# Zero-padded query pairs, untiled scores, a late LN factor, four shared PSUM banks and reordered loads in a chunked-attention and MLP kernel

## The chip, the cores and the metric

The kernel runs on one core of a Trainium2 chip. The metric is the device time of one execution in microseconds (us). Matrix work is done by TensorE (PE, with its weight loads listed as PEld), the rest by VectorE (DVE), ScalarE (ACT) and GpSimd (POOL). DMAs are issued here from POOL (loads from DRAM, which also convert fp32 to fp16) and from SyncE's queue (SP: copies inside the on-chip memory SBUF, and the output).

## The reference

Attention over chunks of 32 positions. Each chunk sees 8 memory keys, 16 positions to its left, itself, and 8 to its right. The result, with the 8 heads of 64 side by side, is the x of a LayerNorm and a two-layer MLP with a residual:

```
B, H, S, D = 4, 8, 768, 64;  chunk, left, right = 32, 16, 8;  n_mem = 8
for each chunk c:
    k_full = concat(mem_k, k[c_start-left : c_end+right]);  v_full likewise
    a = softmax(q_c @ k_full.T / sqrt(D))
    out[c] = a @ v_full
x   = out as (B, S, 512)
xn  = (x - mean(x)) / sqrt(var(x) + 1e-6) * g_ln
y   = x + max(xn @ w_ch1, 0) @ w_ch2          # w_ch1 512 x 2048, w_ch2 2048 x 512
```

## The kernel before

**Attention.** A batch is cut into 12 groups of two chunks (64 queries). For each group, `KT` (L56) holds columns of a block of 72: the left halo, the memory keys, the keys of the group; a score product takes 128 columns from the start of a block and uses 104 of them (KR). `kq_block` (L164) turns two heads of K and Q at a time with 32 PE transposes of 96 rows (L171) into a PSUM tile `att`, of which there are two, each two banks; DVE copies the K half to `KT` (L178), ACT the Q half to `QT` (L182). `scores` (L187) makes, for one group, eight products with a contraction of 64: the even head of a pair lies in rows 0 to 63 and the odd head in rows 64 to 127 of the PE array (tile_position, L194-L199). Each group takes one `att` tile, and two exps of 256 columns (L201) add a band bias that masks what a chunk must not see; the first and the last group have their own biases. `values` (L207) handles two groups (128 positions, tile t): 16 products with V (L213), whose 65th column of ones gives the sums; a reciprocal (L220) and a product (L221) make x, bn_stats and bn_aggr (L228, L229) mean and variance, and four POOL operations (L230 to L241) the normalized xn: minus the mean, plus eps, the power of -1/2, and the pass over x. `turn_x` (L246) transposes xn on PE and copies it to `xT`.

**V.** `V` (L55) has rows for the left halo (0 to 15), the memory values (16 to 23 and 88 to 95), the group (24 to 87) and the right halo (96 to 103). `load_v` (L100) issues one DMA per group from POOL; halos and memory rows are then copied inside SBUF from SP's queue (`load_v_halo`, `load_v_mem`).

**MLP.** The work is cut into eight stages u of 384 positions (three tiles). `up(u, hc)` (L261) makes 128 hidden units with four products of 384 columns (L264) in one of two banks `f1p`; the ReLU goes to `rT` on DVE for even hc (L273) and on ACT for odd hc (L271). `down(u, i, part)` (L279) adds four of the sixteen products of an output tile (L284) in one of two banks `f2p`; after part 3, DVE adds x (L292) and SP issues the output (L293). `scale_w1` (L137) multiplies w1 by g once, 16 passes on DVE (L139).

**Order.** Every engine works through its instructions in the order in which the program writes them. L296 to L363 write the start: batch 0's loads, the identity and masks on POOL, memory keys, four blocks, attention of three tiles, all four `scale_w1`, and the loads of batch 1. Then each stage has 28 steps (L367 to L398): 16 ups, then 12 downs, tile after tile. A plan adds work behind a step: for the next stage's tile i, scores at step 1+7i, values at 5+7i, turn_x at 10+7i; in even stages the four blocks of the next batch at steps 3, 7, 11, 17 and the loads of k and q of the batch after it at step 20; in odd stages V of that batch (12 DMAs from POOL at step 2), its memory columns of KT (on POOL, L158), and the halos. So xn on POOL (L241) stands in one queue with all loads from DRAM.

Of the kernel before, what the change touches and what calls it, by code (L numbers as in the profile page):

```python
# [15 lines left out]
def kernel(  # L16
# [12 lines left out]
    nc = tc.nc  # L29
# [7 lines left out]
    HD = 65  # L37

# [9 lines left out]
    band = sb.tile([128, 3, 2], FP32, name="band")  # L48
    zero6 = sb.tile([128, 3, 2], FP32, name="zero6")
    mhalf = sb.tile([128, 3], FP32, name="mhalf")  # L50
# [6 lines left out]
    QT = [sb.tile([128, 4, S], FP16, name=f"QT{i}") for i in range(2)]  # L57
    AT = [sb.tile([128, H, 64], FP16, name=f"AT{i}") for i in range(4)]
# [6 lines left out]
    mv = [sb.tile([128, 2], FP32, name=f"mv{i}") for i in range(3)]  # L65
    lnc = [sb.tile([128, 3], FP32, name=f"lnc{i}") for i in range(3)]
# [3 lines left out]
    f1p = [ps.tile([128, 384], FP32, name=f"f1p{i}") for i in range(2)]  # L70
    f2p = [ps.tile([128, 512], FP32, name=f"f2p{i}") for i in range(2)]
    turn = {"att": 0, "f1": 0, "f2": 0}

    def slot(kind):
        lst = {"att": att, "f1": f1p, "f2": f2p}[kind]
        turn[kind] = (turn[kind] + 1) % len(lst)
        return lst[turn[kind]]
# [15 lines left out]
    def load_kq(b):  # L93
        for dst, src in ((k16, k), (q16, q)):
            nc.gpsimd.dma_start(
                out=dst[b % 2][:, :, :, :],
                in_=dram(src, b * H * HS, [[512, 96], [HS, H], [1, 512]]),
            )

    def load_v(b, g0, g1):  # L100
        vt = V[b % 2]
        for g in range(g0, g1):
            nc.gpsimd.dma_start(  # L103
                out=vt[24:88, g, :, 0:64],
                in_=dram(v, b * H * HS + 64 * g * D, [[64, 64], [HS, H], [1, 64]]),
            )

    def load_v_halo(b, g0, g1):

        vt = V[b % 2]  # L110
        lo = max(g0, 1)
        nc.sync.dma_start(out=vt[0:16, lo:g1, :, :], in_=vt[72:88, lo - 1 : g1 - 1, :, :])
        hi = min(g1, NG - 1)
        nc.sync.dma_start(out=vt[96:104, g0:hi, :, :], in_=vt[24:32, g0 + 1 : hi + 1, :, :])

    def load_v_mem(b):
# [14 lines left out]
    def load_w2(c):  # L131
        nc.gpsimd.dma_start(
            out=w2c[c],
            in_=dram(moe_w_ch2, c * 512 * 512, [[512, 128], [128 * 512, 4], [1, 512]]),
        )
# [20 lines left out]
    def mem_cols(b):  # L156
        src = memKT[:, 4 * b : 4 * b + 4, :]
        nc.gpsimd.tensor_copy(  # L158
# [5 lines left out]
    def kq_block(b, j):  # L164

        p = slot("att")
        for half, src in ((0, k16), (1, q16)):
            pv = as16(p[:, half, :])
            for r in range(8):
                for par in range(2):  # L170
                    nc.tensor.matmul(  # L171
                        out=pv[64 * par : 64 * par + 64, 96 * r : 96 * r + 96],
                        lhsT=src[b % 2][:, 2 * j + par, r, :], rhs=identity[0:96, 0:96],
                        is_transpose=True, start=True, stop=True,
                        tile_position=(0, 64 * par),
                    )
        pk, pq = as16(p[:, 0, :]), as16(p[:, 1, :])
        nc.vector.tensor_copy(  # L178
            out=free(KT[b % 2], j * KC + 24, [[BLK, NG], [8, 8], [1, 8]]),
            in_=free(pk, 0, [[8, NG], [1, 8], [96, 8]]),  # L180
        )
        nc.scalar.copy(  # L182
            out=free(QT[b % 2], j * S, [[8, 96], [1, 8]]),
            in_=free(pq, 0, [[1, 96], [96, 8]]),
        )

    def scores(b, t):  # L187
        for g in (2 * t, 2 * t + 1):
            cls = 0 if g == 0 else 2 if g == NG - 1 else 1
            p = slot("att")  # L190
            a = AT[g % 4]
            for j in range(4):
                for par in range(2):
                    nc.tensor.matmul(  # L194
                        out=p[:, par, 64 * j : 64 * j + 64],
                        lhsT=KT[b % 2][64 * par : 64 * par + 64, j, BLK * g : BLK * g + 128],
                        rhs=QT[b % 2][64 * par : 64 * par + 64, j, 64 * g : 64 * g + 64],
                        start=(j == 0), stop=(j == 3), tile_position=(64 * par, 0),
                    )  # L199
            for c in range(2):  # L200
                nc.scalar.activation(  # L201
                    out=free(a, 32 * c, [[64, 2], [128, 4], [1, 32]], KR),
                    in_=free(p, 32 * c, [[512, 2], [64, 4], [1, 32]], KR),
                    func=ACTF.Exp, bias=band[0:KR, cls, c : c + 1], scale=0.125,
                )

    def values(b, t, x):  # L207
        p = slot("att")
        for h in range(H):
            for gg in range(2):  # L210
                g = 2 * t + gg
# [3 lines left out]
                    lhsT=AT[g % 4][0:KR, h, :],  # L215
                    rhs=V[b % 2][0:KR, g, h, :],
# [9 lines left out]
        )  # L226
        i = t % 3
        nc.vector.bn_stats(out=bst[i], in_=x)  # L228
        nc.vector.bn_aggr(out=mv[i], in_=bst[i])  # L229
        nc.gpsimd.tensor_scalar(  # L230
            out=lnc[i][:, 0:1], in0=mv[i][:, 0:1], scalar1=-1.0, scalar2=1.0,
            op0=ALU.mult, op1=ALU.mult,
        )
# [195 lines left out]
```

## Time and profile before

| | |
|---|---|
| median of three runs | 303.1 us (302.35 to 304.27) |
| profiled execution, its own time | 303.64 us |
| its span in the profile | 301.9 us |
| PE busy, share of the span | 226.7 us, 75% |
| DVE, POOL, ACT busy | 124.1, 92.4, 79.6 us |
| mean granted PE clock | 0.955 |

The profile is that of one execution. Times in its rows count from the start of the span. In a timeline row stand start, length, engine, line, operation, output <- inputs, shapes and count; in brackets the idle time before it and what ended it. A row with x8 merges eight instructions, and its length reaches to the modelled end of the last, so that the time from one row's start to the next row's start is the better price. Rows of groups end in busy time, mean ns of one, idle time before, and the releaser.

### The profile page before, as it was taken

What the parts mean: (1) busy time and instruction counts of PE and PEld (TensorE: products, weight loads), DVE (VectorE), ACT (ScalarE), POOL (GpSimd) and SP (SyncE); (2) the same over time, 40 slices, a digit from 0 to 9 for tenths busy, and PEclk for the clock granted to TensorE, in tenths of its full rate; (3) what the DMA queues carried; (4) which work ended last, traced back from release to release, by engine and by line L of the source; (5) the groups of instructions that cost most, each with busy time, mean ns of one, the idle gap of its engine ahead of it and who ended that gap; (6) DMA issues with size and microseconds to landing.
All of it is one profiled execution on the core that took longest, in us unless ns stands there. A gap on an engine that the chain in (4) does not pass through costs nothing.

```text
span 301.9 us, 5523 instructions
## 1 busy us (share of the span) xinstructions
PE 226.7 (75%) x2288; PEld 122.4 (41%) x2288; DVE 124.1 (41%) x253; ACT 79.6 (26%) x177; POOL 92.4 (31%) x185
## 2 busy tenths in 40 slices
PE   0073136289997059999998079989998999899994
PEld 0072022145554024455444034455444544444541
DVE  2042374065435015375535034375435445543311
ACT  1026103035224003055314012155224304321300
POOL 8194476250290332210291522220212220221000
PEclk9999999879999759999999759999999999999999
DMA  6999999992069990100169990100010011011001
GB/s 79 169 125 184 157 200 173 147 55 39 35 115 190 83 48 29 64 28 2 37 102 207 86 54 35 72 2 2 35 72 0 3 71 37 0 38 69 0 37 69
DMA packets 41978, 22.26 MB, mean 74 GB/s; under 512 B 27752, under 2 KB 38760, under 8 KB 41880
## 3 DMA queue, kind: packets, MB, share of 16 engines
q0 software_dynamic: 36896, 13.70, 67.5%
q1 hardware_dynamic: 5056, 8.19, 9.9%
q8 instruction: 18, 0.29, 0.5%
q14 instruction: 8, 0.07, 0.1%
HBM read 27.40 MB, written 6.29 MB: 112 GB/s over the span
## 4 chain that ended last, share of the span: by engine, by line
PE 57%; DMA 17%; POOL 8%; DVE 8%; issue 5%; ACT 2%; DVEq 0%; POOLq 0%; ACTq 0%
PE f2p L284 26%; PE f1p L264 23%; DMA q<-in_q_dram 13%; DMA w1c<-in_moe_w_ch_dram 4%; PE att L213 3%; PE att L171 2%; PE att L250 2%; PE att L194 2%; DVE bst L228 2%; DVE xs L221 2%; POOL V L103 2%; DVE KT L178 2%; POOL xn L241 1%; ACT QT L182 1%; POOL lnc L238 1%
## 5 line engine op out<-in xcount | busy, mean ns | idle before, releaser
L264 PE MATMUL f1p<-xT,w1c 128*128 128x384 f16 x512 | 101.4, 341 | 8.9 <-DVE rT L273 5.3
L284 PE MATMUL f2p<-w2c,rT 128*128 128x512 f16 x384 | 87.8, 379 | 0.0
L271 ACT ACTIVATE rT<-f1p 128x384 f16<-128x384 f32 x64 | 31.7, 496 | 151.8 <-PE f1p L264 151.7
L264 PEld LDWEIGHTS <-w1c 128*128 128x128 f16 x512 | 48.9, 101 | 46.0 <-issue 18.9
L273 DVE TENSOR_SCALAR rT<-f1p 128x384 f16<-128x384 f32 x64 | 35.2, 550 | 41.6 <-PE f1p L264 41.5
L284 PEld LDWEIGHTS <-rT 128*128 128x128 f16 x384 | 35.7, 98 | 39.5
L103 POOL DMA_DIRECT2D V<-in_v_dram x48 | 32.3, 685 | 37.8 <-DMA q<-in_q_dram 13.9
L230 POOL TENSOR_SCALAR lnc<-mv 128x1 f32<-128x1 f32 x24 | 4.6, 192 | 127.5 <-DVE mv L229 127.5
L201 ACT ACTIVATE AT<-att,band 104x256 f16<-104x256 f32 x96 | 37.6, 480 | 9.5 <-PE att L194 9.5
L250 PE MATMUL att<-identity,xn 128*128 128x128 f16 x96 | 10.5, 239 | 31.7 <-POOL xn L241 31.6
L292 DVE TENSOR_TENSOR osb<-f2p,xs 128x512 f32<-128x512 f32 x24 | 16.6, 692 | 40.8 <-PE f2p L284 40.8
L255 DVE COPY xT<-att 128x512 f16<-128x512 f16 x24 | 10.1, 420 | 46.2 <-PE att L250 46.2
L182 ACT COPY QT<-att 128x768 f16<-128x768 f16 x16 | 12.8, 800 | 46.4 <-DVE KT L178 46.4
L178 DVE COPY KT<-att 128x768 f16<-128x768 f16 x16 | 15.3, 956 | 17.0 <-PE att L171 17.0
L250 PEld LDWEIGHTS <-xn 128*128 128x128 f16 x96 | 6.5, 104 | 38.9 <-POOL xn L241 38.1
L241 POOL TENSOR_SCALAR xn<-xs,lnc 128x512 f16<-128x512 f32 x24 | 18.9, 786 | 2.6
L221 DVE TENSOR_TENSOR xs<-att,rec 128x512 f32<-128x512 f32 x24 | 16.6, 691 | 1.0 <-DVE rec L220 0.2
L228 DVE BATCH_NORM_STATS2 bst<-xs 128x6 f32<-128x512 f32 x24 | 16.7, 694 | 0.8
L194 PE MATMUL att<-QT,KT 64*128 64x64 f16 x384 | 11.6, 198 | 5.6 <-ACT QT L182 3.8
L238 POOL TENSOR_TENSOR lnc<-lnc,mhalf 128x1 f32<-128x1 f32 x24 | 13.4, 558 | 2.0
L194 PEld LDWEIGHTS <-KT 64*128 64x128 f16 x384 | 8.1, 98 | 13.5 <-issue 13.1
L213 PEld LDWEIGHTS <-AT 104*64 104x64 f16 x384 | 9.0, 120 | 10.5 <-issue 8.5
(36 smaller groups left out, 91.8 us busy)
## 6 DMA issues: line engine op xcount, KB each, us to landing
out_dram<-osb SPq DMA_DIRECT2D x24, 256.0 KB, 2.0
k<-in_k_dram POOLq DMA_DIRECT2D x4, 768.0 KB, 9.1
q<-in_q_dram POOLq DMA_DIRECT2D x4, 768.0 KB, 14.2
V<-in_v_dram POOLq DMA_DIRECT2D x48, 64.0 KB, 12.5
w1c<-in_moe_w_ch_dram POOLq DMA_DIRECT2D x4, 512.0 KB, 9.6
w2c<-in_moe_w_ch_dram POOLq DMA_DIRECT2D x4, 512.0 KB, 13.9
V<-memv SPq DMA_DIRECT2D x8, 97.5 KB
V<-V SPq DMA_DIRECT2D x3, 178.8 KB
```

What stands on the lines that cost most here:

```text
L103: nc.gpsimd.dma_start(out=vt[24:88, g, :, 0:64], in_=dram(v, b * H * HS + 64 * g * D, [[64, 64], [HS, H], [1, 64]]),)
L178: nc.vector.tensor_copy(out=free(KT[b % 2], j * KC + 24, [[BLK, NG], [8, 8], [1, 8]]), in_=free(pk, 0, [[8, NG], [1, 8], [96, 8]]),)
L194: nc.tensor.matmul(out=p[:, par, 64 * j : 64 * j + 64], lhsT=KT[b % 2][64 * par : 64 * par + 64, j, BLK * g : BLK * g + 128], rhs=QT[b % 2 ...
L201: nc.scalar.activation(out=free(a, 32 * c, [[64, 2], [128, 4], [1, 32]], KR), in_=free(p, 32 * c, [[512, 2], [64, 4], [1, 32]], KR), func= ...
L221: nc.vector.tensor_tensor(out=x.rearrange("p (a h d) -> p a h d", a=2, h=4), in0=free(p, 0, [[512, 2], [HD, 4], [1, 64]]), in1=free(r, 0, ...
L228: nc.vector.bn_stats(out=bst[i], in_=x)
L241: nc.gpsimd.tensor_scalar(out=xn[i], in0=x, scalar1=lnc[i][:, 0:1], scalar2=lnc[i][:, 2:3], op0=ALU.add, op1=ALU.mult,)
L250: nc.tensor.matmul(out=pv[:, 128 * dt : 128 * dt + 128], lhsT=xn[i][:, 128 * dt : 128 * dt + 128], rhs=identity, is_transpose=True, start= ...
L264: nc.tensor.matmul(out=p, lhsT=w1c[hc // 4][:, dt, 128 * (hc % 4) : 128 * (hc % 4) + 128], rhs=xT[u % 2][:, dt, :], start=(dt == 0), stop= ...
L271: nc.scalar.activation(out=rT[u % 2][hc], in_=p, func=ACTF.Relu)
L273: nc.vector.tensor_scalar(out=rT[u % 2][hc], in0=p, scalar1=0.0, scalar2=None, op0=ALU.max)
L284: nc.tensor.matmul(out=p, lhsT=rT[u % 2][hc][:, 128 * i : 128 * i + 128], rhs=w2c[hc // 4][:, hc % 4, :], start=(hc == 0), stop=(hc == 15),)
```

## The change

- **Scores.** Q goes to `QZ`: for each group and pair of heads 128 columns, the even head's 64 with zeros in rows 64 to 127, the odd head's 64 with zeros in rows 0 to 63. One product with all 128 rows then gives both heads' scores: four per group without tile_position instead of eight with it. `scores` does both groups of a tile in one `att` tile, with two exps of 512 columns. ACT copies Q in two halves of 64 rows. The zeros are cleared once at the start by DVE. One band bias is left: for the first and last group the rows outside the sequence have zeros in V and in its ones column (`tail1`).
- **LN.** xn is x minus the mean only. The factor (var + 1e-6)^(-1/2) is made in `root` on POOL and multiplied in at the output (ReLU lets a positive factor of a row through): L292 becomes one scalar_tensor_tensor. In the first stages the subtraction is done by DVE, later by POOL (`on_pool`).
- **MLP.** `f1p` and `f2p` become four shared banks `mm`. `rT` is kept once instead of twice. w2 is loaded with 2048 contiguous elements per partition, so hidden unit 4p+i of a part lies at place (p, i), and `up` takes its weights from w1 with a step of four elements.
- **Loads and order.** K, Q of batches 0 and 1 are loaded and turned in two parts (rows 0 to 63, then 64 to 95; CUT); V of batches 2 and 3 is loaded in eight DMAs by head, spread over steps of stages 2 and 4; the identity and masks are written ahead of V's loads; `mem_cols` moves from POOL to DVE; `scale_w1` 1 to 3 move into stage 0; the steps of stages 0, 1 and 2 get their own plan.

The diff, cut to its core:

```
-    QT = [sb.tile([128, 4, S], FP16, name=f"QT{i}") for i in range(2)]
-    AT = [sb.tile([128, H, 64], FP16, name=f"AT{i}") for i in range(4)]
+    QZ = [sb.tile([128, 4, NG, 2, 64], FP16, name=f"QZ{i}") for i in range(2)]
+    AT = [sb.tile([128, 2, H, 64], FP16, name=f"AT{i}") for i in range(3)]
-    rT = [[sb.tile([128, 384], FP16, name=f"rT{i}_{hc}") for hc in range(16)] for i in range(2)]
+    rT = [sb.tile([128, 384], FP16, name=f"rT{hc}") for hc in range(16)]
-    f1p = [ps.tile([128, 384], FP32, name=f"f1p{i}") for i in range(2)]
-    f2p = [ps.tile([128, 512], FP32, name=f"f2p{i}") for i in range(2)]
+    mm = [ps.tile([128, 512], FP32, name=f"mm{i}") for i in range(4)]
...
     def mem_cols(b):
-        nc.gpsimd.tensor_copy(
+        nc.vector.tensor_copy(
...
-        nc.scalar.copy(
-            out=free(QT[b % 2], j * S, [[8, 96], [1, 8]]),
-            in_=free(pq, 0, [[1, 96], [96, 8]]),
-        )
+        for par in range(2):
+            rows = slice(64 * par, 64 * par + 64)
+            o = free(QZ[b % 2][rows, j, g0, par, :], 0, [[128, ng], [8, 8], [1, 8]])
+            i = free(pq[rows, :], 0, [[8, ng], [1, 8], [n, 8]])
+            nc.scalar.copy(out=o, in_=i)
...
+        p = slot("att")
+        a = AT[t % 3]
+        for gg in range(2):
+            g = 2 * t + gg
             for j in range(4):
+                nc.tensor.matmul(
+                    out=p[:, gg, 128 * j : 128 * j + 128],
+                    lhsT=KT[b % 2][:, j, BLK * g : BLK * g + 128],
+                    rhs=QZ[b % 2][:, j, g, :, :],
+                    start=True, stop=True,
+                )
+        for c in range(2):
+            nc.scalar.activation(
+                out=free(a, 32 * c, [[512, 2], [64, 8], [1, 32]], KR),
+                in_=free(p, 32 * c, [[512, 2], [64, 8], [1, 32]], KR),
+                func=ACTF.Exp, bias=band[0:KR, c : c + 1], scale=0.125,
+            )
...
+        if on_pool:
...
+            root(t, xi)
+        else:
+            nc.vector.tensor_scalar(
+                out=xn[i], in0=x, scalar1=m[:, 0:1], scalar2=None, op0=ALU.subtract,
+            )
...
     def up(u, hc):
+        p = slot("mm")[:, 0:384]
+        c, i = hc // 4, hc % 4
         for dt in range(4):
+            w = w1c[c][:, dt, :]
             nc.tensor.matmul(
+                out=p, lhsT=free(w, i, [[4, 128]]), rhs=xT[u % 2][:, dt, :],
...
-            nc.vector.tensor_tensor(out=o, in0=p, in1=xs[t % 9], op=ALU.add)
+            nc.vector.scalar_tensor_tensor(
+                out=o, in0=p, scalar=rstd[t % 9], in1=xs[t % 9], op0=ALU.mult, op1=ALU.add,
+            )
...
+        if u == 0:
+            for c in range(1, 4):
+                at(4 * c - 2, scale_w1, c)
             for j in range(4):
+                at(15, kq_block, 0, j, CUT, 96)
+            attend(((15, 16, 19), (15, 17, 21), (16, 18, 23)))
+            at(24, mem_cols, 1)
+            at(24, v_mem, 1)
+        elif u == 1:
+            for j in range(4):
+                at(10 + j, kq_block, 1, j, 0, CUT)
+            at(12, v_before, 1, 1, 6)
+            at(12, v_after, 1, 0, 5)
+            attend(((16, 20, 24), (18, 22, 26), (20, 24, 27)))
+            for which in range(2):
+                at(24, load_kq, 1, which, CUT, 96)
+            for g in range(6, NG):
+                at(25, load_v_group, 1, g)
...
+            for which in range(2):
+                at(27, load_kq, 2, which)
+        elif u + 1 < NU:
+            attend(tuple((1 + 7 * i, 5 + 7 * i, 10 + 7 * i) for i in range(3)))
+            if u == 2:
+                plan.clear()
+                for j in range(4):
+                    at(j, kq_block, 1, j, CUT, 96)
+                attend(((5, 10, 15), (9, 14, 19), (13, 18, 24)))
+                for j in range(4):
+                    at((17, 20, 22, 25)[j], kq_block, 2, j)
...
+            if u in (2, 4):
+                bn = u // 2 + 1
+                for h in range(H):
+                    at(6 + 2 * h, load_v_head, bn, h)
+                at(24, mem_cols, bn)
+                at(24, v_mem, bn)
+                at(27, v_before, bn, 1, NG)
+                at(27, v_after, bn, 0, NG - 1)
+            if u == 3:
+                for which in range(2):
+                    at(2 + which, load_kq, 3, which)
         for step in range(28):
             if step < 16:
                 up(u, step)
+            elif u == 0:
+                down(u, (step - 16) % 3, (step - 16) // 3)
             else:
                 down(u, (step - 16) // 4, (step - 16) % 4)
```

At the start the new order is: on POOL the loads of mem_k and of rows 0 to 63 of k and q, the identity, the masks, V of groups 0 to 5 and its right halo, w1, the rest of k and q, V of groups 6 to 11, w2; on DVE the clears of V, KT and QZ, then `tail1`; then memory keys and columns, four blocks of rows 0 to 63, attention of three tiles with one `scale_w1` between the second and the third xT.

More of the change, by code (lines that the diff above doesn't have):

```diff
@@ L132, in load_w2 @@
         nc.gpsimd.dma_start(
-            out=w2c[c],
-            in_=dram(moe_w_ch2, c * 512 * 512, [[512, 128], [128 * 512, 4], [1, 512]]),
+            out=w2c[c], in_=dram(moe_w_ch2, c * 512 * 512, [[2048, 128], [1, 2048]])
         )
@@ L162, in mem_cols, with kq_block @@
         )
-    def kq_block(b, j):
+    def kq_block(b, j, lo=0, hi=96):
+        n, g0, ng = hi - lo, lo // 8, (hi - lo) // 8
         p = slot("att")
@@ L187, in scores @@
     def scores(b, t):
[L188 to L191, printed above, removed]
+        p = slot("att")
+        a = AT[t % 3]
+        for gg in range(2):
+            g = 2 * t + gg
             for j in range(4):
[L193 to L204, printed above, removed]
-                )
@@ L208, in values @@
+    def values(b, t, xi, on_pool):
+        x = xs[xi]
         p = slot("att")
@@ L284, in down @@
             nc.tensor.matmul(
-                out=p, lhsT=rT[u % 2][hc][:, 128 * i : 128 * i + 128],
+                out=p, lhsT=rT[hc][:, 128 * i : 128 * i + 128],
                 rhs=w2c[hc // 4][:, hc % 4, :],
@@ L372, in at, with attend @@
             plan.setdefault(step, []).append((fn, args))
-        if u + 1 < NU:
-            for i in range(3):
+        def attend(i_steps):
+            for i, (s0, s1, s2) in enumerate(i_steps):
                 t = 3 * half + i
-                at(1 + 7 * i, scores, b1, t)
-                at(5 + 7 * i, values, b1, t, xs[(3 * (u + 1) + i) % 9])
-                at(10 + 7 * i, turn_x, u + 1, i)
-        if u % 2 == 0 and u // 2 + 1 < B:
-            bn = u // 2 + 1
-            for j in range(4):
-                at((3, 7, 11, 17)[j], kq_block, bn, j)
-            if bn + 1 < B:
-                at(20, load_kq, bn + 1)
```

247 lines of the change are left out of this document (138 added, 109 removed).

## The prediction

> **What bounds the kernel now.** I read the busy times by stage first. A stage u runs from its first up product to the next stage's; the eight follow each other, columns being window, length, busy time (with counts) of PE, PEld, DVE, ACT, POOL, then granted clock, DMA share, GB/s.
>
> ```profile
> 47.70:87.50 39.80, 32.40 (x349) 17.15 (x349) 15.58 (x29) 11.32 (x24) 14.24 (x27) 0.91 0.91 85
> 87.50:126.40 38.90, 26.42 (x222) 13.32 (x221) 12.67 (x26) 8.20 (x20) 12.38 (x24) 0.87 1.41 93
> 126.40:155.90 29.50, 28.44 (x349) 15.69 (x348) 16.13 (x30) 11.20 (x24) 7.98 (x16) 1.00 0.11 31
> 155.90:193.50 37.60, 27.15 (x221) 13.75 (x220) 12.88 (x26) 8.20 (x20) 12.38 (x24) 0.86 1.28 96
> 193.50:223.10 29.60, 28.56 (x350) 15.75 (x349) 16.13 (x30) 11.20 (x24) 5.11 (x12) 1.00 0.08 28
> 223.10:249.50 26.40, 24.90 (x222) 12.87 (x221) 12.58 (x26) 8.20 (x20) 5.12 (x12) 1.00 0.08 31
> 275.90:301.90 26.00, 21.99 (x113) 10.74 (x111) 7.19 (x12) 3.93 (x8) 0.00 (x0) 1.00 0.11 41
> ```
>
> Stage 6 equals stage 5. Undisturbed stages (4 to 7) are bound by PE. Stages 1 and 3 have stage 5's work but last 38.9 and 37.6 against 26.4 us: 23.7 us lost, with the clock at 0.87. The chain that ended last says to what:
>
> ```profile
> 3.00 11.55 DMA q<-in_q_dram
> ...
> 153.82 14.32 DMA q<-in_q_dram
> ...
> 172.86 0.54 POOL KT L158
> ...
> 174.56 0.78 POOL xn L241
> 175.39 0.61 PE att L250 x4
> ```
>
> POOL issues loads in order and then makes xn. A V load stands until q has landed, xn behind it, and PE behind xn. The start, by the timeline, loses more:
>
> ```profile
> 14.84 0.67 POOL L103 DMA_DIRECT2D V<-in_v_dram  x1 [3.83 <-DMA q<-in_q_dram]
> 16.06 0.09 DVE L311 MEMSET memv<- 8x32 f16 x1 [11.86 <-DMA memv<-in_mem_v_dram]
> 16.14 0.56 PE L149 MATMUL att<-identity,memk 8*128 8x8 f16 x16 [16.14 <-POOL identity masks.py:199]
> 21.46 0.68 SPq L114 DMA_DIRECT2D V<-V  x1
> 28.82 0.65 PE L213 MATMUL att<-V,AT 104*64 104x65 f16 x16 [1.74 <-DMA w1c<-in_moe_w_ch_dram]
> 37.71 0.77 POOL L241 TENSOR_SCALAR xn<-xs,lnc 128x512 f16<-128x512 f32 x1
> 41.87 5.47 DVE L139 TENSOR_SCALAR w1c<-w1c,g_col 128x512 f16<-128x512 f16 x16
> 47.72 2.72 PE L264 MATMUL f1p<-xT,w1c 128*128 128x384 f16 x8 [2.79 <-DVE xT L255]
> 51.87 0.67 POOL L103 DMA_DIRECT2D V<-in_v_dram  x1 [1.33 <-DMA w2c<-in_moe_w_ch_dram]
> 59.27 0.85 PE L171 MATMUL att<-identity,q 96*64 96x96 f16 x16 [3.77 <-DMA q<-in_q_dram]
> ```
>
> The identity waits behind a V load until 15.8; first xn stands behind w2 issues until 37.7; four w1 scalings (5.47) stand in DVE ahead of the last xT; then stage 0 waits for batch 1's k and q. At 51.87 a V load comes free on a w2 load: all of w2 has landed.
>
> **Inside a stage** the PE timeline prices everything:
>
> ```profile
> 129.49 0.53 PE L171 MATMUL att<-identity,k 96*64 96x96 f16 x16
> ...
> 130.30 1.47 PE L264 MATMUL f1p<-xT,w1c 128*128 128x384 f16 x8
> ...
> 223.06 1.46 PE L264 MATMUL f1p<-xT,w1c 128*128 128x384 f16 x8
> 224.46 0.41 PE L194 MATMUL att<-QT,KT 64*128 64x64 f16 x16
> 224.80 2.96 PE L264 MATMUL f1p<-xT,w1c 128*128 128x384 f16 x16
> 227.69 0.45 PE L213 MATMUL att<-V,AT 104*64 104x65 f16 x16
> ...
> 230.69 0.81 PE L264 MATMUL f1p<-xT,w1c 128*128 128x384 f16 x4 [1.14 <-DVE rT L273]
> ...
> 246.63 0.40 PE L250 MATMUL att<-identity,xn 128*128 128x128 f16 x4
> 246.87 2.75 PE L284 MATMUL f2p<-w2c,rT 128*128 128x512 f16 x12
> ...
> 275.86 11.67 PE L264 MATMUL f1p<-xT,w1c 128*128 128x384 f16 x64
> 287.37 10.52 PE L284 MATMUL f2p<-w2c,rT 128*128 128x512 f16 x48
> ```
>
> I count from one start to the next. A down product takes 10.52/48 = 0.219 us; three quarters of its width 0.164, so 64 up products 10.5. They take 11.5 in stage 7.
>
> **Part by part.**
>
> *Four shared banks.* I read that 1.0 us as waits for the two f1 banks, besides the 1.14 and some 0.4 us of visible waits in stages like 5. With four banks an eviction may be late by three up groups (2.0 us), more than the values chain holds DVE. Gain 1.0 in stage 7, about 1.9 elsewhere. The single set of rT costs nothing: rT's first four are last read three down groups (2.6 us) before the next stage rewrites them.
>
> *Scores.* Sixteen tiled products take 0.34 us. Four untiled 128-wide ones with their own loads take 0.24 (the transposes), so eight 0.48: +0.14 per pair, 24 pairs, +3.4. The Trainium skill (TensorEngine Tiling (Array Packing), When to Use Tiling) recommends row tiling for a contraction of 64, up to twofold: by it the pair would cost 0.68 and the sum be some 5 us more; the transposes' row decides. ACT's half as many, twice as wide exps cost no more (rows below), off PE.
>
> *Zero-padded Q* doubles ACT's copies:
>
> ```profile
> L264 PEld LDWEIGHTS <-w1c 128*128 128x128 f16 x512 | 48.9, 101 | 46.0 <-issue 18.9
> L201 ACT ACTIVATE AT<-att,band 104x256 f16<-104x256 f32 x96 | 37.6, 480 | 9.5 <-PE att L194 9.5
> L271 ACT ACTIVATE rT<-f1p 128x384 f16<-128x384 f32 x64 | 31.7, 496 | 151.8 <-PE f1p L264 151.7
> L228 DVE BATCH_NORM_STATS2 bst<-xs 128x6 f32<-128x512 f32 x24 | 16.7, 694 | 0.8
> L182 ACT COPY QT<-att 128x768 f16<-128x768 f16 x16 | 12.8, 800 | 46.4 <-DVE KT L178 46.4
> L297 DVE MEMSET V<- 32x512 f16 x2 | 1.0, 485 | 0.9 <-PEq L413 0.9
> L314 DVE MEMSET KT<- 128x64 uint32 x2 | 0.2, 112 | 0.0
> ```
>
> +0.8 us per block, covered because ACT is busy 11 of 29 us; uncovered, 3 us per such stage. A block costs PE 0.81 us (129.49 to 130.30). Splitting batches 0 and 1 issues the same 32 transposes on fewer columns: I charge a full 0.8, four more blocks in stages 0 and 2 each.
>
> *Strided w1 weights.* up now reads every fourth column. No row shows a strided load. Bounds: nothing, up to four times the row's 101 ns if each element costs what four neighbours do now. It is hidden while it stays below the product's 164 ns. I take nothing, being nearest to the only row, and keep the other end as a rival. The Trainium skill pulls both ways here. Its page SBUF — State Buffer (Door 1: The DMA port swizzle) asks for two hits in a 16-byte line, which a step of four halves just gives, and by that the sum stays. Its page TensorE: Matmul & The Clock Gate (Weight-path perf modes) has the fast load read two 16-bit weights at a time, packed or strided; if a step of four loses that pairing, the sum is rival A's.
>
> *Work moved to DVE.* The four w1 scalings stay 1.4 us each, but only the first stands before stage 0; the others follow steps 2, 6 and 10. There each holds the evictions behind it, and PE behind these, for 1.4 us, less than the three banks' lead; if its part of w1 were late, all of that would wait; I take it as landed, since in the old order POOL, which waits for w1 before it issues w2, was through with all of that by 37.7, and step 10 comes near 44. The key columns (0.54 us on POOL) go to DVE: once ahead of the first blocks, where they count in full, and three times under downs, where DVE is half idle.
>
> *LN factor.* xn loses the wait for the root; the root follows it. In stages 2 on it was hidden (five steps between values and turn). The output operation stays one DVE pass over 512 elements. In the first two stages xn moves to DVE, out of POOL's queue: about 0.5 us each, between the 0.34 of a w1 pass (5.47/16) and the 0.69 of bn_stats.
>
> *Loads.* V of batches 2 and 3 goes out as eight issues spread between steps 6 and 20, after q has long been issued, and k and q of batch 3 a stage earlier than needed: stages 1 and 3 lose their stall. In stages 2 and 4 each xn may stand behind one issue (under a microsecond, five steps of slack), and behind a landing only where an issue comes less than eight after k or q: the last two of stage 2, some 14 us (the q row above) after q. Late next: q's last rows for batch 1, issued four steps before stage 2 transposes them. I charge 1 us there and 0.7 us for V's halos at stage 3.
>
> **The start, step by step.** Identity no longer waits. Two thirds of k and q land at 3.0 + 2/3 × 11.55 = 10.7. DVE first clears V (four clears of 0.485 and smaller ones, some 3.5 us from 0.9 on), KT (0.4), then four Q halves of 3072 halves each: at 0.95 ns an element 1.5 us if packed in pairs (KT's row is uint32), 2.9 if not; free at 10.5 or 16. I take 10.5. V loads wait for this too: the memv row shows that a write to column 64 and a load to columns 0–63 are ordered. Four blocks at 1.2 us of ACT end near 17, exps near 20. Values need halos and memory rows of V; memory values land near 18, and a halo took 7.4 us (21.46 to 28.82): 25.5, bounds 20 to 29. Then 0.7 of values, three DVE chains of 2.3 (0.2 + 0.7 + 0.7 + 0.2 + 0.5), two xT copies (0.8), one scaling (1.4), one copy (0.4): stage 0 begins at 35.8 instead of 47.7.
>
> Stage 0: ups 10.5, plus 2.0 for the halved clock (first eight took 2.72 where 1.40 is usual) and 0.3: to 48.6. At step 15 come four half blocks (4.2), then downs 10.5, values 1.1, scores 1.5, turns 0.7, and 1.2 of waits because three scores and values follow at once: to 67.8. All of w2 landed by 51.9 before; the same bytes go ahead of it now, five us later at worst, and its first quarter is needed at 54.
>
> Stages, new against old. 1: 28.6 (24.6 + four blocks + 0.8 for late turns) against 38.9. 2: 32.4 (24.6, eight blocks 6.4, the late q 1.0, ACT's longer copies 0.4) against 29.5. 3: 25.3 (24.6 and the halos) against 37.6, the clock's loss gone with the stall. 4: 28.0 (24.6, four blocks, 0.2) against 29.6. 5 and 6: 24.6 (26.4 − 1.9 + 0.4 for scores − 0.3: eight ups ahead of a tiled group take 1.40, not 1.31, and three tiled groups go) against 26.4. 7: 20.9 and the same 4.0 tail. Sum 67.8 + 28.6 + 32.4 + 25.3 + 28.0 + 49.2 + 24.9 = 256.2 span against 301.9. That execution took 303.6 in all, 1.7 outside the span, and the median is 303.1: **258 us**.
>
> **Rivals.**
> A. The strided load doubles, one of each two neighbours read being of no use: 202 ns instead of 101, so each up product stretches by 38 ns, 512 × 38 = +19.5: 277. For: no strided load is in the trace. Against: a load has 63 ns to spare under its product now (164 − 101), so anything short of that is free.
> B. The other side: the strided load takes four times the row, all four neighbours being read for one, 404 ns; 512 × 240 = +123, giving 381. It decides against the change from 254 ns on (45 us / 512 = 88 ns above 164).
> C. The start stays bound by loads and DVE: memsets unpacked (free at 16) and halos late, stage 0 at 44: 266.
> D. The banks do not do what I say (the 0.18 us is the products' own rate): 1.0 in stage 7 and up to 1.9 in each other stays, 8 to 14 us: 270. Against: the visible DVE wait at 230.69.
>
> **Chances.** Forecast 0.55 (249 to 265), C 0.15, D 0.12, A 0.12, B 0.06. The range 248 to 275 holds the first three; A's and B's 0.18 lie above. About 1% is what a measurement can tell from no change. Only B is slower: faster 0.94, same 0.01, slower 0.05 (a mild B could land on no change).
>
> **What would show it.** Right: the first up product near 36 us; no idle time above 3 us of PE after it; stages 5 and 6 near 24.6; 64 ups of stage 7 in 10.5; eight score products in about 0.5. Wrong: PEld on w1c far above 101 ns; stage 0 starting beyond 42; POOL's xn standing behind the V issues in stage 2 or 4.

## The result, and the profile after

The changed kernel takes 287.7 us in the median (287.3 to 288.4), the kernel before 303.7 (302.4 to 305.2) beside it: ratio 0.948, 95% interval 0.942 to 0.953. It is faster by 16 us where the prediction had 45, and 287.7 lies above its range. The profiled execution has a span of 285.8 us against the forecast 256.2. An execution that took over 1.5% longer than the fastest of its kernel, at a lower granted clock, is left out of the medians and ranges below (one of e1, the profiled one, and one of e5).

First the stages, by the same view as before (window, length, busy time with counts of PE, PEld, DVE, ACT, POOL, granted clock, DMA share, GB/s), of the changed kernel:

```profile
44.40:78.95 34.55, 32.38 (x324) 18.11 (x324) 18.71 (x45) 10.54 (x22) 8.83 (x15) 0.95 0.95 89
78.95:107.95 29.00, 27.62 (x325) 16.86 (x324) 17.82 (x35) 12.12 (x22) 6.97 (x12) 1.00 0.34 69
107.95:140.80 32.85, 31.07 (x453) 19.35 (x453) 17.79 (x34) 15.92 (x29) 14.71 (x26) 1.00 1.29 124
140.80:174.00 33.20, 25.94 (x198) 15.21 (x197) 12.71 (x26) 8.44 (x16) 4.87 (x12) 0.90 0.39 77
174.00:202.65 28.65, 28.16 (x325) 17.48 (x324) 16.44 (x31) 13.75 (x22) 10.92 (x20) 1.00 0.72 56
202.65:231.70 29.05, 26.04 (x198) 15.13 (x197) 12.71 (x26) 7.56 (x14) 4.87 (x12) 0.94 0.19 45
231.70:260.50 28.80, 28.31 (x326) 17.60 (x325) 16.26 (x30) 13.75 (x22) 4.86 (x12) 1.00 0.08 29
260.50:285.80 25.30, 20.77 (x113) 11.72 (x110) 7.37 (x12) 3.93 (x8) 0.00 (x0) 1.00 0.11 42
```

Three things are to be seen. Stage 0 begins at 44.4, not 35.8. Stages 3 and 5 have PE busy for 26 us but last 33.2 and 29.05. Stage 6 is long in another way: PE is busy nearly all the time, and its counts (326 PE instructions, 13.75 us of ACT) are those of stage 4 (325 and 13.75), which makes K and Q of another batch; after batch 3 there is none. Set beside the prediction's sum (the last column is a mended kernel, told below):

| | forecast | changed | mended (e8_all) |
|---|---|---|---|
| stage 0 begins | 35.8 | 44.4 | 34.5 |
| stage 0 | 32.0 | 34.55 | 34.03 |
| stage 1 | 28.6 | 29.00 | 29.01 |
| stage 2 | 32.4 | 32.85 | 33.28 |
| stage 3 | 25.3 | 33.20 | 24.26 |
| stage 4 | 28.0 | 28.65 | 29.67 |
| stage 5 | 24.6 | 29.05 | 24.27 |
| stage 6 | 24.6 | 28.80 | 24.29 |
| stage 7 and tail | 24.9 | 25.30 | 25.19 |
| span | 256.2 | 285.8 | 258.5 |

Of the 29.6 us that were missed, 8.6 lie at the start, 7.9 in stage 3, 4.4 in stage 5, 4.2 in stage 6, and 2.5 in stage 0. The chain that ended last, of the changed kernel, shows what the first three hang on (start, length, what):

```profile
23.04 0.76 SPq L135
23.85 10.57 DMA V<-memv
...
114.49 5.87 DMA V<-V
...
134.80 7.49 DMA k<-in_k_dram
...
143.07 9.34 DMA V<-V
...
199.78 4.93 DMA V<-in_v_dram
...
205.68 4.36 DMA V<-V
```

Four times the chain runs through a copy inside SBUF that SP issues: memory rows or halos of V, which PE's values (L231) need. It lasts 10.57, 5.87, 9.34 and 4.36 us, in the order of the rows. The second lies in stage 2, where PE waits only 1.41 us for it. The PE timeline shows what the others cost, and the blocks of stage 6:

```profile
34.51 0.65 PE L231 MATMUL att<-V,AT 104*64 104x65 f16 x16 [14.87 <-DMA V<-memv]
44.39 8.22 PE L291 MATMUL mm<-xT,w1c 128*128 128x384 f16 x32 [1.10 <-DVE xT L279]
...
59.34 0.42 PE L188 MATMUL att<-identity,k 32*64 32x32 f16 x16
...
152.55 0.65 PE L231 MATMUL att<-V,AT 104*64 104x65 f16 x16 [7.26 <-DMA V<-V]
153.13 3.54 PE L291 MATMUL mm<-xT,w1c 128*128 128x384 f16 x12
...
203.95 0.61 PE L212 MATMUL att<-QZ,KT 128*128 128x128 f16 x8
204.40 2.76 PE L291 MATMUL mm<-xT,w1c 128*128 128x384 f16 x16
210.17 0.45 PE L231 MATMUL att<-V,AT 104*64 104x65 f16 x16 [3.01 <-DMA V<-V]
...
234.82 0.53 PE L188 MATMUL att<-identity,k 96*64 96x96 f16 x16
...
260.35 10.56 PE L291 MATMUL mm<-xT,w1c 128*128 128x384 f16 x64
270.75 10.52 PE L309 MATMUL mm<-w2c,rT 128*128 128x512 f16 x48
```

The row at 234.82 is a transpose of K in stage 6. The last two rows hold a part of the forecast that came true: 64 up products take 270.75 − 260.35 = 10.40 us.

Theory: the sum was right but for two things, namely copies inside SBUF that are issued late and into the stream of POOL's loads, and the blocks for a batch that doesn't exist. Rivals: the strided loads, the untiled scores or the shared banks cost or bring something other than forecast.

### The profile page after: what moved, and what is told of

Same layout as the page of the kernel before. It is cut to its first block, busy times and chain, and to the rows that moved or that the text cites. A ratio compares the mean times of both kernels' runs of the same rounds, so it can differ in the third digit from the quotient of the medians.

```text
span 285.8 us, 5905 instructions
## 1 busy us (share of the span) xinstructions
PE 232.1 (81%) x2480; PEld 141.4 (49%) x2480; DVE 139.7 (49%) x285; ACT 95.6 (33%) x169; POOL 78.6 (28%) x154
## 4 chain that ended last, share of the span: by engine, by line
PE 46%; DMA 20%; issue 12%; POOL 10%; DVE 8%; SPq 2%; ACT 1%; POOLq 0%; DVEq 0%; ACTq 0%
PE mm L291 22%; PE mm L309 16%; DMA V<-V 7%; DMA V<-in_v_dram 7%; DMA V<-memv 4%; POOL V L111 3%; DMA k<-in_k_dram 3%; PE att L188 2%; PE att L231 2%; POOL xn L253 2%; POOL V L105 2%; PE att L212 2%; POOL rstd L268 2%; ACT QZ L204 1%; DVE bst L246 1%
## 5 line engine op out<-in xcount | busy, mean ns | idle before, releaser
L291 PE MATMUL mm<-xT,w1c 128*128 128x384 f16 x512 | 98.6, 342 | 2.6 <-DVE xT L279 2.0
L309 PE MATMUL mm<-w2c,rT 128*128 128x512 f16 x384 | 90.3, 382 | 0.0
L296 ACT ACTIVATE rT<-mm 128x384 f16<-128x384 f32 x64 | 31.2, 491 | 105.8 <-PE mm L291 55.4
L298 DVE TENSOR_SCALAR rT<-mm 128x384 f16<-128x384 f32 x64 | 35.3, 551 | 35.7 <-PE mm L291 35.6
L204 ACT COPY QZ<-att 64x768 f16<-64x768 f16 (+2 forms) x56 | 34.1, 609 | 47.4 <-DVE KT L196 46.6
L219 ACT ACTIVATE AT<-att,band 104x512 f16<-104x512 f32 x48 | 30.1, 684 | 21.9 <-PE att L212 21.6
L317 DVE SCALAR_TENSOR_TENSOR osb<-mm,rstd,xs 128x512 f32<-128x512 f32 x24 | 18.0, 750 | 34.5 <-PE mm L309 26.6
L231 PE MATMUL att<-V,AT 104*64 104x65 f16 x384 | 11.8, 208 | 26.9 <-DMA V<-memv 14.9
L196 DVE COPY KT<-att 128x768 f16<-128x768 f16 (+2 forms) x28 | 20.4, 728 | 18.1 <-PE att L188 15.1
L231 PEld LDWEIGHTS <-AT 104*64 104x64 f16 x384 | 9.4, 119 | 35.3 <-issue 31.3
L105 POOL DMA_DIRECT2D V<-in_v_dram x24 | 16.3, 686 | 23.6 <-DMA w1c<-in_moe_w_ch_dram 8.9
L212 PE MATMUL att<-QZ,KT 128*128 128x128 f16 x192 | 16.3, 234 | 2.3 <-ACT QZ L204 2.3
## 6 DMA issues: line engine op xcount, KB each, us to landing
w1c<-in_moe_w_ch_dram POOLq DMA_DIRECT2D x4, 512.0 KB, 10.5
k<-in_k_dram POOLq DMA_DIRECT2D x2, 768.0 KB, 10.4
```

Source lines behind the costliest of these rows:

```text
L105: nc.gpsimd.dma_start(out=V[b % 2][24:88, g, :, 0:64], in_=dram(v, b * H * HS + 64 * g * D, [[64, 64], [HS, H], [1, 64]]),)
L196: nc.vector.tensor_copy(out=free(KT[b % 2], j * KC + 24 + BLK * g0, [[BLK, ng], [8, 8], [1, 8]]), in_=free(pk, 0, [[8, ng], [1, 8], [n, 8]]),)
L204: nc.scalar.copy(out=o, in_=i)
L212: nc.tensor.matmul(out=p[:, gg, 128 * j : 128 * j + 128], lhsT=KT[b % 2][:, j, BLK * g : BLK * g + 128], rhs=QZ[b % 2][:, j, g, :, :], sta ...
L219: nc.scalar.activation(out=free(a, 32 * c, [[512, 2], [64, 8], [1, 32]], KR), in_=free(p, 32 * c, [[512, 2], [64, 8], [1, 32]], KR), func= ...
L231: nc.tensor.matmul(out=p[64 * gg : 64 * gg + 64, h // 4, c0 : c0 + HD], lhsT=AT[t % 3][0:KR, gg, h, :], rhs=V[b % 2][0:KR, 2 * t + gg, h, ...
```

## The experiments

e1 to e8 start from the changed kernel, e9 and e10 from e8_all, e11 from the kernel before. Each was timed beside the kernel before; ratios are to that.

**Guard (e1_guard).** The plan of the old kernel made blocks only for a batch that exists.

```
-            elif u % 2 == 0:
+            elif u % 2 == 0 and u // 2 + 1 < B:
```

> Only edit to the changed kernel: the four K/Q blocks that stage 6 makes for a fifth batch, which does not exist, are left out (their results are never read, so the output is the same). Theory: they stand on PE's path, so stage 6 falls from 28.8 us to stage 5's undisturbed 24.6 and the whole from 287.7 to about 283.5. Rival: stage 6 is long because of something else (ACT, the values chain) and the blocks fill gaps: under 1 us.

282.9 us (281.3 to 283.9), ratio 0.927 (0.919 to 0.936): 4.8 below the changed kernel. In its PE timeline the last twelve downs of stages 5 and 6 give the length of stage 6, 256.02 − 231.74 = 24.28 us, where the same rows of the changed kernel give 257.76 − 229.09 = 28.67:

```profile
231.74 2.75 PE L309 MATMUL mm<-w2c,rT 128*128 128x512 f16 x12
...
256.02 2.75 PE L309 MATMUL mm<-w2c,rT 128*128 128x512 f16 x12
```

**K and Q of batch 3 ten steps later (e2_kq3_late).** Nothing about the halos is touched, only what runs beside them.

```
-                    at(2 + which, load_kq, 3, which)
+                    at(12 + which, load_kq, 3, which)
```

> Only edit: k and q of batch 3 are issued at steps 12 and 13 of stage 3 instead of 2 and 3, so that on POOL they stand behind stage 3's first xn and no longer right behind batch 2's V. Theory (the V halo copies are slow because they share the DMA engines with those two loads): the copy ahead of stage 3 takes 4 to 5 us instead of 9.3, PE's wait there falls from 7.3 to 2 to 3 us, stage 3 loses its half clock, total 281 to 283. Rival (the copy is slow by itself, for its few partitions): 9.3 and 7.3 stay, total 287 to 288.

282.0 us (280.9 to 282.9), ratio 0.925 (0.918 to 0.932). The SP and PE timelines of this kernel:

```profile
142.64 0.67 SPq L129 DMA_DIRECT2D V<-V  x1
```

```profile
147.19 0.45 PE L231 MATMUL att<-V,AT 104*64 104x65 f16 x16 [2.33 <-DMA V<-V]
147.57 2.14 PE L291 MATMUL mm<-xT,w1c 128*128 128x384 f16 x12
```

The same copy is over some 4.5 us after its issue instead of 9.3, and the twelve products behind it run in 2.14 us instead of 3.54. So at stage 3 the copy's length was that of sharing DMA engines with k and q.

**Memory rows first (e3_mem_first).** The load of mem_v, which the changed kernel issues behind V of groups 0 to 5, goes ahead of V's loads, the ones of memv16 are set early, and SP issues the memory rows ahead of the halos.

```
     make_identity(nc, identity)
+    nc.gpsimd.dma_start(out=memv16[:, :, :, 0:64], in_=dram(mem_v, 0, ...))
...
+    v_mem(0)
     v_before(0, 1, 2)
     v_after(0, 0, 2)
...
     v_after(0, 4, 5)
-    v_mem(0)
```

> Only edit: at the start mem_v is loaded right after the identity, and the copies of the memory rows into V go first in SP's queue, ahead of the halos. Theory (the memory rows, issued last at 23 us into a full DMA stream, hold the first values until 34.5): first values near 25, stage 0 begins at 37 to 39 instead of 44.4, total 281 to 283. Rival 1 (any copy issued while w1 streams in lands late, so the halos take the place of the memory rows): stage 0 begins above 41, gain under 3 us. Rival 2 (w2's landing sets the end of stage 0): stage 0 begins earlier but the total stays within 1 us of 287.7.

278.8 us (277.1 to 280.5), ratio 0.915 (0.907 to 0.922), more than expected. SP and PE timelines:

```profile
12.42 1.62 SPq L135 DMA_DIRECT2D V<-memv  x2
```

```profile
25.26 0.65 PE L231 MATMUL att<-V,AT 104*64 104x65 f16 x16 [5.08 <-DMA V<-V]
35.13 8.00 PE L291 MATMUL mm<-xT,w1c 128*128 128x384 f16 x32 [1.10 <-DVE xT L279]
```

First values at 25.3 and stage 0 at 35.1: the prediction had 25.5 and 35.8. The halos are last now. The agreement is partly luck: by the chain of this kernel the halo that PE waits for goes out at 19.93 and takes 5.20 us, where the prediction had 18 and 7.4.

**Halos early (e5_halo_early).** All V heads go out at step 1 (two of batch 2 at step 14), and the copies inside SBUF at step 20.

```
-                    at(6 + 2 * h, load_v_head, bn, h)
+                    at(14 if u == 2 and h > 5 else 1, load_v_head, bn, h)
...
-                at(24, v_mem, bn)
-                at(27, v_before, bn, 1, NG)
-                at(27, v_after, bn, 0, NG - 1)
+                at(20, v_mem, bn)
+                at(20, v_before, bn, 1, NG)
+                at(20, v_after, bn, 0, NG - 1)
```

> Changed kernel, but V of batches 2 and 3 is issued at step 1 of stages 2 and 4 (two of batch 2's heads at step 14), and the copies of memory rows and halos at step 20 instead of 24 and 27, ahead of the stage's last two outputs in SP's queue. Theory (the copies come late because the last V head stands on POOL behind the third xn and the copies on SP behind the last output): stage 5's wait of 3.0 us goes and the stage falls from 29.0 to 24.7; stage 3's wait falls from 7.3 to 1 to 3, as k and q of batch 3 still share the engines; total 279 to 281. Rival (the copies are too slow wherever they are issued): stage 5 keeps 2 us or more of wait, total above 284.

274.3 us (274.0 to 276.0), ratio 0.901 (0.893 to 0.909), again below what was expected. The wait for halos is gone in stages 3 and 5. It takes back 13.4 us, and 7.9 + 4.4 were missed there: an earlier issue cures both stages, without any change to what runs beside the copies' old place. e2 and e5 thus take away the same wait in stage 3, and their gains don't add.

**The clears (e6_tail_first).** The ones column that V's loads wait for goes ahead of the clears of KT and QZ; the second batch's clears go behind the second scores.

```
-    for i in range(2):
-        nc.vector.memset(KT[i]...)
-        nc.vector.memset(QZ[i]...)
+    clear(0)              # behind tail1 and the ones of V
...
     scores(0, 1)
+    clear(1)
```

> Changed kernel, but DVE copies the ones column (which V's loads wait for) ahead of the clears of KT and QZ, and clears batch 1's only after the second scores. Theory (V's loads stand 6.5 us behind the clears): V loads start near 5.7 instead of 11.8, first values at 28 to 30 instead of 34.5, stage 0 begins at 38 to 40, total 282 to 284. Rival (the memory rows land when w1 has, whenever V came): first values stay above 33 and the total within 2 us of 287.7.

284.7 us (282.3 to 286.1), ratio 0.932 (0.924 to 0.940): 3 us, a little less than expected. In its profile the first values come at 29.26 and stage 0 begins at 39.20, both as expected and 5.2 us earlier than in the changed kernel, with PE still waiting 9.77 us for the memory rows. Stage 2 gives back some 2 of these 5.2 us (34.9 us long instead of 32.85), since there the products behind a wait for V's halos run slowly (PE timeline):

```profile
115.61 0.45 PE L231 MATMUL att<-V,AT 104*64 104x65 f16 x16 [1.81 <-DMA V<-V]
116.00 3.40 PE L291 MATMUL mm<-xT,w1c 128*128 128x384 f16 x12
```

So the clears matter through the time at which V's loads go out, and don't explain the start by themselves.

**Two and two banks (e4_two_banks).** Rival D, that the banks bring nothing. The downs of stage 0 go tile after tile here, since two banks can't hold three tiles.

```
-    mm = [ps.tile([128, 512], FP32, name=f"mm{i}") for i in range(4)]
+    f1p = [ps.tile([128, 512], FP32, name=f"f1p{i}") for i in range(2)]
+    f2p = [ps.tile([128, 512], FP32, name=f"f2p{i}") for i in range(2)]
...
-                down(u, (step - 16) % 3, (step - 16) // 3)
+                down(u, (step - 16) // 4, (step - 16) % 4)
```

> The changed kernel with two PSUM banks for up and two for down again, and stage 0's downs tile after tile, since three at once would need three banks. Theory (two banks make the up products wait for evictions): stage 7's 64 up products take 11.5 us instead of 10.4, stages 4 to 6 are 1 to 1.9 us longer each, total 8 to 14 us more, 296 to 302. Rival (the time per product came down for another reason, such as the strided weights): stages 4 to 7 stay, total 287 to 290.

298.1 us (297.6 to 299.3), ratio 0.978 (0.971 to 0.986): the banks, with the order of stage 0's downs that needs them, are worth 10.4 us here. Stage 0, where that order changed too, is only 0.8 us longer in the profile; stages 4 to 7 are 1.1 to 2.8 longer, 4 and 6 more than expected. PE's list of waits has 6.1 us in nine waits for ACT's evictions of rT, and none in the changed kernel. In stage 7 the ups take 282.45 − 270.88 = 11.57 us again, by the PE timeline:

```profile
270.88 11.74 PE L292 MATMUL f1p<-xT,w1c 128*128 128x384 f16 x64
282.45 2.75 PE L310 MATMUL f2p<-w2c,rT 128*128 128x512 f16 x12
```

**Weights in a row (e7_contiguous_w1).** The rivals A and B: w1 is read without a step, and w2 goes back to rows of 512.

```
-                lhsT=free(w, i, [[4, 128]])
+                lhsT=w[:, 128 * i : 128 * i + 128]
```

> Changed kernel with the hidden units in their old order: w1's columns are loaded into the array as neighbours, w2 comes in rows of 512 elements. Theory (the step of four is hidden under the products): PEld on w1c falls from 117 ns to about 101, the 64 up products of stage 7 stay at 10.4 us, total 286.5 to 288.5. Rival (the stride costs PE time): total below 285.

286.0 us (284.7 to 287.1), ratio 0.937 (0.930 to 0.945), an interval that overlaps the changed kernel's. The total lies between what was expected (286.5 to 288.5) and the rival's (below 285), and doesn't decide; the trace does. The weight loads by line, of the changed kernel and then of this one:

```profile
L291 PEld LDWEIGHTS <-w1c 128*128 128x128 f16 x512 | 56.3, 117 | 31.7 <-issue 7.5 <-DVE w1c L154 2.3
```

```profile
L292 PEld LDWEIGHTS <-w1c 128*128 128x128 f16 x512 | 48.7, 101 | 37.3 <-issue 6.6 <-DVE w1c L155 3.8
```

A step of four makes a load 16 ns longer, all of it under the products: the 64 ups of stage 7 take 10.40 us in both.

**All mends together (e8_all).** e1, e2, e3, e5 and e6.

> The five mends together: no blocks for a fifth batch, k and q of batch 3 late, memory rows first, ones column ahead of the clears, V and halos early. Theory (separate waits on one path): the gains add up to some 4 + 6 + 9 + 3 + 4, total 258 to 264, stages 3, 5 and 6 at 24.6 us each, no PE wait above 1.5 us after stage 0 begins. Rival (stage 0's end hangs on w2's landing, or the earlier loads collide): total above 268.

260.15 us (259.5 to 260.2), ratio 0.852 (0.845 to 0.859), span 258.5. That is the fastest kernel of the study together with e10 below, and close to the blind forecast of 258, which was made for another kernel. One thing was expected that didn't come: stage 2 keeps a PE wait of 1.87 us, for V's halos of batch 1 (110.53). Stage 4 is 1.0 us longer than in the changed kernel, 0.80 of it a wait for q of batch 3, which is now issued late. Its stages 3, 5 and 6:

```profile
130.82:155.08 24.26, 24.26 (x197) 14.68 (x196) 12.62 (x26) 8.46 (x16) 9.20 (x18) 1.00 0.42 76
...
184.75:209.02 24.27, 24.27 (x197) 14.70 (x196) 12.62 (x26) 7.57 (x14) 4.86 (x12) 1.00 0.14 48
209.02:233.31 24.29, 24.29 (x198) 14.70 (x197) 12.62 (x26) 7.52 (x14) 4.86 (x12) 1.00 0.09 34
```

PE is busy for the whole of each.

**Tiled scores in it (e9_tiled_scores).** e8_all with sixteen row-tiled products per pair and four exps of 256 columns instead of two of 512.

```
-                    lhsT=KT[b % 2][:, j, BLK * g : BLK * g + 128],
-                    rhs=QZ[b % 2][:, j, g, :, :],
+                        lhsT=KT[b % 2][64 * par : 64 * par + 64, j, BLK * g : BLK * g + 128],
+                        rhs=QZ[b % 2][64 * par : 64 * par + 64, j, g, par, :],
+                        tile_position=(64 * par, 0),
```

> e8_all with the scores as 16 row-tiled products of 64 columns again (reading the same zero-padded Q, one head of a pair in each half of the array, the heads in different banks) and four exps of 256 columns for a pair of groups. Theory (untiling costs 0.45 us instead of 0.34 for a pair of groups and nothing else): PE gains some 0.1 us at 24 places, total 257 to 259 against 260.2. Rival 1 (tiling doubles the rate): the scores fall to 0.22 us, total about 255. Rival 2 (the untiled form pays by fewer mode switches and by fewer exps): total 260 to 263.

266.1 us (264.5 to 268.1), ratio 0.876 (0.869 to 0.881): 5.9 slower than e8_all, where 1 to 3 faster was expected. The expectation fell. Its stages 0, 3, 4, 5 and 6, by the same view:

```profile
34.41:71.60 37.19, 32.19 (x348) 17.56 (x348) 18.73 (x45) 11.57 (x28) 13.01 (x24) 0.91 1.13 108
...
132.83:157.13 24.30, 24.30 (x221) 13.98 (x220) 12.62 (x26) 9.22 (x22) 9.21 (x18) 1.00 0.41 75
157.13:189.48 32.35, 29.94 (x350) 17.26 (x349) 16.59 (x31) 14.43 (x28) 8.10 (x17) 0.95 1.17 73
189.48:213.78 24.30, 24.30 (x222) 14.01 (x220) 12.62 (x26) 8.20 (x20) 4.88 (x12) 1.00 0.13 47
213.78:238.07 24.29, 24.29 (x221) 14.00 (x220) 12.62 (x26) 8.20 (x20) 4.89 (x12) 1.00 0.09 34
```

In the three stages that PE fills, tiled and untiled scores last the same within 0.04 us. The loss lies in stage 0 (3.2) and stage 4 (2.7); stage 2 gives 1.1 back. Stage 0 shows a gap in the second tiled group for which the profile names no releaser, and stage 4 a wait for q that is 0.84 us longer and leaves the next eight ups at half speed:

```profile
54.18 0.58 PE L213 MATMUL att<-QZ,KT 64*128 64x64 f16 x15 [0.36 <-ACT QZ L204]
57.28 0.21 PE L213 MATMUL att<-QZ,KT 64*128 64x64 f16 x1 [2.52 <-issue]
...
157.13 1.46 PE L294 MATMUL mm<-xT,w1c 128*128 128x384 f16 x8
158.53 0.41 PE L213 MATMUL att<-QZ,KT 64*128 64x64 f16 x16
158.87 1.49 PE L294 MATMUL mm<-xT,w1c 128*128 128x384 f16 x8
...
162.46 0.53 PE L188 MATMUL att<-identity,q 96*64 96x96 f16 x16 [1.64 <-DMA q<-in_q_dram]
162.92 2.75 PE L294 MATMUL mm<-xT,w1c 128*128 128x384 f16 x8
```

The wait for q is no price of the score products. The gap lies within a group of them, and its cause isn't known; the edit also changes the exps, and no run here parts the two. Whether the tiled form brings gap and wait about each time or this execution met them by chance stays open; the four timed runs are all slower than each of e8_all's.

**Batch 1 whole (e10_whole_kq1).** e8_all with k and q of batch 1 loaded and turned in one piece.

```
-                at(10 + j, kq_block, 1, j, 0, CUT)
+                at(10 + j, kq_block, 1, j)
...
-                    at(j, kq_block, 1, j, CUT, 96)
```

> e8_all with batch 1's k and q loaded whole at the start and turned whole in stage 1, so that the four half blocks in stage 2 go. Theory (a half block costs PE 0.65 us against 0.8 for a whole one, so splitting batch 1 costs four times 0.65 plus what the two blocks of 0.15 differ): stage 2 loses 2.5 to 3 us, stage 1 gains 0.5, total 257 to 258.5 against 260.2. Rival (the larger load holds w2 or V back, or ACT's longer copies hold stage 1): total 259.5 or more.

259.6 us (258.9 to 260.6), ratio 0.854 (0.849 to 0.858): no difference that can be told from e8_all, and in the range of the rival. By its PE timeline stage 1 runs from 69.68 to 100.60 and stage 2 to 129.11: stage 2 is 4.8 us shorter than in e8_all, more than expected, but stages 0, 1 and 4 are 1.3, 1.9 and 1.35 longer, stage 4 through a wait of 2.15 us for q instead of 0.80.

**The banks alone in the kernel before (e11_before_banks).**

```
-    f1p = [ps.tile([128, 384], FP32, name=f"f1p{i}") for i in range(2)]
-    f2p = [ps.tile([128, 512], FP32, name=f"f2p{i}") for i in range(2)]
+    mm = [ps.tile([128, 512], FP32, name=f"mm{i}") for i in range(4)]
```

> The kernel before with the four shared banks alone. Theory (two f1 banks cost 1.0 us in stage 7 and up to 1.9 in each other stage, as in the prediction; two banks in the changed kernel cost 10.4 us in all): total 290 to 295 against 303.7, stages 5 and 6 at 24.2 to 24.6 instead of 26.4. Rival (the start and the load stalls absorb it): less than 5 us, total above 298.

299.3 us (297.9 to 301.6), ratio 0.985 (0.979 to 0.991): 4.4 us, less than expected. The waits of PE in this kernel, then in the kernel before (who waits, for whom, us in total, times, longest):

```profile
PE att L249 <- POOL xn L240: 36.2, 7, 12.2
```

```profile
PE att L250 <- POOL xn L241: 31.6, 5, 11.3
...
PE f1p L264 <- DVE rT L273: 5.3, 6, 1.1
```

The wait for DVE's evictions is gone from the new list, and the wait for xn has grown by nearly as much. There POOL's queue of loads sets the end of stages 1 and 3, so that what PE gains ahead of it is waited out again. By stages, only 5, 6 and 7 are clearly shorter (24.92, 24.93 and 24.86 us instead of 26.40, 26.40 and 26.04). Stage 4 isn't, for another reason: PE now waits 1.06 us for ACT's copy of Q, where it waited 0.34 for an eviction and 0.66 for that copy. The same banks are worth 10.4 us in the changed kernel (e4).

## Why the prediction was right, and where it was wrong

**Right: what bounds the work.** PE does fill an undisturbed stage, and it stays at 24.3 us (24.6 forecast). Stages 1, 2, 4 and 7 came within 0.7 us, stage 2 partly by luck: it charged 1.0 us for q's last rows, for which PE doesn't wait, and nothing for V's halos, for which PE waits 1.41. The stalls for xn in stages 1 and 3 went, as did the start's wait for the identity; DVE's clears let V's loads go at 11.8 (10.5 forecast). Once the causes below are mended and the clears moved, e8_all's 258.5 us of span answer to 256.2. That the two are so near is in part a balance: stages 0 and 4 are 2.0 and 1.7 longer there than forecast, and its stage 0 begins 1.3 earlier.

**Wrong: "Values need halos and memory rows of V; memory values land near 18, and a halo took 7.4 us (21.46 to 28.82): 25.5."** The terms are there, but the order is not followed through. The memory rows are the last of SP's copies, issued at 23.0, and by then w1 streams: 10.6 us, and values at 34.5. The upper bound of 29 took no account of SP's order beside POOL's stream. e3, which moves only these rows and their load, gets 25.3 and 35.1 (25.5 and 35.8 forecast).

**Wrong: "0.7 us for V's halos at stage 3", and none at stage 5.** I looked at POOL's queue and at xn, and not at what follows a V load: halos go out at 142.5 and 143.1, behind an output of the stage before, PE wants them at 145.3 (152.55 − 7.26), and k and q of batch 3, issued at 134.8 and 135.6, are still in flight. The wait was 7.3 us and another 3.0 in stage 5; slow products behind each of them made it 7.9 and 4.4. The "Late next" of the prediction was the right question, and I answered it with q and these 0.7 us. e2 shows the sharing, e5 the late issue.

**Wrong: stage 6 at 24.6.** I overlooked in the diff that the new plan makes blocks in every even stage from the second on, where the old one asked whether the next batch exists. Four blocks of 1.1 us; e1 takes them away. The 0.81 us that I charged for a block leaves out that the eight ups ahead of one take 1.39 us instead of 1.30 (233.43 to 234.82 in the changed kernel) and that PE waits 0.24 and 0.26 us for ACT in such a stage; the rest stays open.

**Mis-sized: stage 0's ups.** The prediction charged 2.0 us for the slow beginning; up to the first block it takes 59.34 − 44.40 = 14.9 us instead of 12.8. The first 32 products take 8.22 us, where 0.163 each would be 5.2: 3.0 rather than 2.0. The other 32 are 1.5 us over, with two waits of 0.27 and 0.26 for DVE's scalings of w1, for which the sum names no term. That stays in e8_all (14.3 us), and how the excess divides stays open.

**Scores.** Eight untiled products take 0.45 us (203.95 to 204.40), 0.48 forecast. But the surcharge of 3.4 us over tiled ones isn't there: in e9 a tiled pair takes 158.87 − 158.53 = 0.34, and the eight ups ahead of it 1.40, where they take 1.30 ahead of an untiled pair in e8_all; so whole stages are equal. I had counted that 0.1 us only in the lines on stages 5 and 6. The Trainium skill (TensorEngine Tiling (Array Packing), When to Use Tiling) advises row tiling at a contraction of 64; here, in stages that PE fills, it brought nothing.

**Rivals.** A and B fell (e7). B's turning point of 254 ns should read 252, 164 + 88. D fell (e4: without the banks 10.4 us come back, within the 8 to 14 that D gave). C had stage 0 at 44 and its price near right, but not for its reasons, unpacked clears and late halos: a clear of half of one QZ took 1.34 us in the trace, nearer the 1.5 of a packed one, and the copies that came last were the memory rows. e6 shows that the place of the clears matters all the same, for 5.2 us of the start. C knew nothing of stages 3, 5 and 6.

## What to carry to other kernels

After moving loads, follow each one to the copy that depends on it and to who waits for that: a small copy inside SBUF that is issued last can be held up by the streams beside it (9.34 us instead of 4.41 for the same copy here). Read a rewritten schedule for the conditions it has lost, and compare the instruction counts of each stage with what it should do. A gain on an engine is worth its full size only in stages where that engine sets the end: the same banks brought 4.4 us in the kernel before and 10.4 in the changed one.

## What the runs showed of the hardware

- A copy inside SBUF from SP's queue took 4.36 us (the changed kernel, stage 5) and 4.41 (e2, stage 3) with no load from POOL in flight, and 5.20 (e3, start), 5.87, 9.34 and 10.57 us (the changed kernel) beside loads that POOL had issued.
- A wait can slow PE beyond its own length (the granted clock is 0.90 and 0.94 in stages 3 and 5 of the changed kernel), but in these traces the length of the wait alone doesn't tell when. Behind waits of 1.19, 1.41, 1.87 and 2.33 us for V (e3, the changed kernel, e8_all, e2) the next twelve ups took 2.14 us. Behind 1.81 us (e6, shown above) they took 3.40, and behind 2.62 us (e5) and longer ones 3.20 to 4.03. Of two waits for q, one of 1.64 us (e9, shown above) was followed by eight ups in 2.75 us, and a longer one of 2.15 (e10) by eight in 1.49. The Trainium skill (TensorE: Matmul & The Clock Gate, HAM oscillation — how this bites in real kernels) warns of idle gaps above some 3.4 us; here slow products also followed waits of 1.64, 1.81 and 2.62 us. What decides between 1.6 and 2.4 us stays open.
- Weight loads with a step of four elements took 117 ns (the changed kernel) against 101 ns without a step (e7), hidden under products of 163 ns.
